# A feed-forward kernel whose second weight matrix is stored by even and odd columns and read back in alternation

## The chip, the core and the metric

The kernel runs on one core of one Trainium2 chip. The metric is the device time of one execution in microseconds (us). Before the change it is 949.09 us, the median of three runs (948.34 to 950.35).

## What is computed

Eight batches of eight heads, 576 tokens, head size 64. Half of the heads attend to the last 32 tokens, the other half to every 32nd token. The heads' outputs, side by side, are a row `x` of 512 numbers, and each row then goes through a normalised two-layer network with a residual:

```python
scores = where(mask_of_head, q @ k.T / 8, -1e9)
x = softmax(scores) @ v                     # [8, 576, 512] after joining the heads
xn = (x - mean(x)) / sqrt(var(x) + 1e-6) * g_ln
out = x + relu(xn @ w_ch1) @ w_ch2          # w_ch1 [512, 2048], w_ch2 [2048, 512]
```

The network is the larger part: 4608 tokens by 512 by 2048, twice.

## The kernel before

**Tiles and precision.** The 4608 tokens are cut into 9 chunks of 512 (`c`), the 2048 hidden columns into 16 blocks of 128 (`f`). Each weight and each activation is kept as two `fp32r` tiles, a high part and a low part that is the float32 value less the high part. A product of two such pairs takes three matmuls: high by high, low by high and high by low.

**One step `(c, f)`.** `ffn1` (L566 to L581) makes the 128 hidden columns of block `f` for the 512 tokens of chunk `c`: 12 matmuls into the PSUM tile `ph` (L575 eight, L579 four). ScalarE writes the high part `hh` (L563), VectorE the low part `hl` (L564). `ffn2` (L583 to L591) multiplies them by rows `128 f` to `128 f + 127` of the second matrix: for each of four blocks of 128 tokens three matmuls into `po`, `hh` by `w2h`, `hh` by `w2l`, `hl` by `w2h`, all on L589. In these the activations are the stationary operand (128 columns, loaded anew for each matmul) and the 512 columns of the second matrix are the moving operand, streamed past it. Over the whole program `ffn2` issues 9 x 16 x 12 = 1728 matmuls, and `ffn1` as many. `ffn2` of one step is issued after `ffn1` of the next, so that TensorE works while ScalarE and VectorE make `hh` and `hl`.

**Where the weight tiles come from.** The object `Split` turns each loaded block of the two matrices into the two parts. Its methods run on ScalarE (`scaled`, `low`), VectorE (`magnitude`, `sign`, `centred`) and GpSimd (`by_g`, `chunks_sum`). The last, `two_parts(i)`, makes the tile that the matmuls read: `i = 0` for the first matrix, `i = 1` for the second. ScalarE writes the high part (L241), GpSimd subtracts it from the full value to get the low part (L242). All 32 calls fall in the program's opening and in chunk 0; from chunk 1 on both matrices lie ready in SBUF. The tile of a block of the second matrix has 128 partitions by 2 parts by 512 columns of 4 bytes, so that one part is 2048 contiguous bytes in a partition.

**Attention.** The attention of the next batch (scores, exponentials, transposes and products of L375 to L472) is cut into pieces and placed, in a list written out by hand, between the matmuls of the network. Within each engine the instructions run in the order in which the program issues them.

**Names in the profile.** `po` is the accumulator of `ffn2`, `ph` that of `ffn1`; `w` is a weight tile of either matrix (L241 and L242 write it, 16 times each for each matrix); `r` is the weight's full value before the split; `xh` and `xl` are the two parts of the transposed activations, written on L489 and L491 with the tokens of the strided heads put back in order as they are written; `cm` is a small matmul of column means (L227), which waits for GpSimd's sum (L222).

Of the kernel before, what the change touches and what calls it, by code (L numbers as in the profile page):

```python
# [8 lines left out]
F32 = mybir.dt.float32  # L9
# [3 lines left out]
AF = mybir.ActivationFunctionType  # L13
ALU = mybir.AluOpType
# [6 lines left out]
def kernel(  # L21
# [10 lines left out]
    nc = tc.nc  # L32
# [50 lines left out]
    for jj in range(4):  # L83
        mrow = mask_l[STR * jj:STR * (jj + 1)]
        nc.gpsimd.affine_select(
            out=mrow, in_=mrow, pattern=[[1, 64]], base=-1,
            channel_multiplier=-1, compare_op=ALU.is_ge, fill=FILL)
        nc.gpsimd.affine_select(
            out=mrow, in_=mrow, pattern=[[-1, 64]], base=STR,
# [5 lines left out]
    for c in range(2):  # L95
        for r in range(3):
            msk = mask_s[64 * c:64 * (c + 1), NB * r:NB * (r + 1)]
            nc.gpsimd.affine_select(
                out=msk, in_=msk, pattern=[[-1, NB]], base=-NB * r,
                channel_multiplier=1, compare_op=ALU.is_ge, fill=FILL)  # L100
            nc.gpsimd.affine_select(
                out=msk, in_=msk, pattern=[[0, NB]], base=NB * r + NB - 1,
# [25 lines left out]
    def w_tile(i, f, shape, dtype, name):  # L128
        return w_pools[int(f >= NF2)].tile(shape, dtype, tag=f"w{i}_{f}", name=f"{name}{i}_{f}")
# [47 lines left out]

    staged, w1s, w2s = {}, {}, {}

    class Split:  # L180
        def __init__(self, f):
            self.f = f
            ws = staged.pop(f)
            self.bits = [t.rearrange("p (f t) -> p f t", t=2) for t in ws]
            self.bytes = [t.bitcast(U8).rearrange("p (f b) -> p f b", b=8) for t in ws]
            self.p, self.w = [None, None], [None, None]
# [47 lines left out]
        def two_parts(self, i):  # L234
            w = (self.wg, self.w[1])[i]
            t = w_tile(i + 1, self.f, [P, 2, DM], F32R, "w")
            (w1s, w2s)[i][self.f] = t
            if i == 1 and self.f == NFC - 1:

                w_pools[1].tile([P, PAD], F32, name="pad")  # L240
            nc.scalar.activation(out=t[:, 0], in_=w, func=AF.Copy)  # L241
            nc.gpsimd.tensor_tensor(out=t[:, 1], in0=w, in1=t[:, 0].bitcast(F32), op=ALU.subtract)  # L242

# [336 lines left out]

    def ffn2(c, f, h, po):  # L583
        hh, hl = h
        w2h, w2l = (w2s[f][:, i] for i in range(2))
        for i in range(NT):
            cs = slice(i * P, (i + 1) * P)
            for n, (hx, w) in enumerate(((hh, w2h), (hh, w2l), (hl, w2h))):
                nc.tensor.matmul(  # L589
                    po[i], hx[:, cs], w,  # L590
                    start=(f == 0 and n == 0), stop=(f == NFC - 1 and n == 2))  # L591
# [19 lines left out]
    a, b, c, d = first  # L611
# [110 lines left out]
    for c in range(NCHUNK):  # L722
# [18 lines left out]
        for f in range(NFC):  # L741
# [41 lines left out]
            if c == 0 and f == 1:  # L783
                ffn2(c, 0, prev, po)
# [6 lines left out]
            elif c + 1 == B:  # L791
                i = f // 2 - 1
# [9 lines left out]
            if prev is not None and (c or f > 1):  # L802
                ffn2(c, f - 1, prev, po)
# [6 lines left out]
            for i in scales.get(f, []):  # L810
                xres[i].append(x_scale(xres[i][0], f"{c}_{i}"))
            prev = h
        ffn2(c, NFC - 1, prev, po)
        finish(c, po, xres)

# [42 lines left out]
```

## Time and profile before

| | before |
|---|---|
| median of the runs | 949.09 us (948.34 to 950.35) |
| the profiled execution's own time | 949.45 us |
| its span, first to last instruction | 947.4 us |
| TensorE busy with matmuls | 916.7 us (97%) |
| VectorE, ScalarE, GpSimd busy | 388.9, 223.2, 143.4 us |
| mean granted TensorE clock | 0.993 |

A row of a group names line, engine, operation, output and input, the shape of both, the count, then busy time in us and the mean ns of one; behind the second bar stands the idle time of the engine just before these instructions and what ended it. Matmuls overlap in the pipeline, so the mean ns of one is longer than the distance from one to the next; distances are read from the starts in the timeline.

### The profile page before, as it was taken

To read this page: it belongs to the slowest core of one execution; us is meant where nothing else is said; L and a number is where in the kernel's file an instruction comes from. 1 tells how busy PE (TensorE), PEld (TensorE's weight loads), DVE (VectorE), ACT (ScalarE), POOL (GpSimd) and SP (SyncE) were. 2 spreads that over 40 slices of the span, in tenths; PEclk is the share of its full clock that TensorE was granted. 3 is DMA by queue.
4 is the path that set the end of the run, shared out by engine and by line. 5 is a ranking of instruction groups with operands and counts; after the bars stand their busy time and mean duration, and the time that the engine had idled before them with its cause. 6 is when DMAs were issued, how large, how long until landed. Compare 5 with 4: busy or idle time off the path is not lost.

```text
span 947.4 us, 18698 instructions
## 1 busy us (share of the span) xinstructions
PE 916.7 (97%) x7984; PEld 747.8 (79%) x7984; DVE 388.9 (41%) x685; ACT 223.2 (24%) x375; POOL 143.4 (15%) x180
## 2 busy tenths in 40 slices
PE   6589999999999999999999999999999999999996
PEld 5468877888888888888888888888888888888885
DVE  5768777334433344334433443334432331122112
ACT  4666751212111221111112112121112111111110
POOL 3477771000010001001100100000100000000000
PEclk9899999999999999999999999999999999999999
DMA  9999646424332352334253333243311130002001
GB/s 192 233 221 274 188 112 135 93 49 88 95 69 41 69 109 61 72 74 85 73 87 60 82 90 63 52 87 73 84 25 50 50 110 25 1 1 89 0 1 45
DMA packets 241666, 80.72 MB, mean 85 GB/s; under 512 B 192304, under 2 KB 234928, under 8 KB 241584
## 3 DMA queue, kind: packets, MB, share of 16 engines
q1 hardware_dynamic: 238688, 78.35, 36.5%
q10 hardware_dynamic: 2896, 1.18, 0.8%
q8 instruction: 63, 1.03, 0.5%
q14 instruction: 19, 0.16, 0.1%
HBM read 60.03 MB, written 19.46 MB: 84 GB/s over the span
## 4 chain that ended last, share of the span: by engine, by line
PE 92%; DVE 3%; DMA 2%; issue 1%; ACT 1%; SPq 1%; DVEq 0%; POOL 0%; POOLq 0%; ACTq 0%
PE po L589 41%; PE ph L575 27%; PE ph L579 13%; PE pp L416 2%; PE av L430 2%; PE px L472 2%; PE sp L387 2%; PE sp L375 1%; PE av L439 1%; DMA rows<-in_k_dram 1%; DMA raw<-in_q_dram 1%; DVE p L200 1%; PE t L315 1%; DVE r L206 1%; DVE x L595 0%
## 5 line engine op out<-in xcount | busy, mean ns | idle before, releaser
L589 PE MATMUL po<-w,hh 128*128 128x512 f32 x1152 | 367.6, 400 | 0.0
L564 DVE SCALAR_TENSOR_TENSOR hl<-ph,hh 128x512 fp32r<-128x512 f32 x144 | 99.5, 691 | 485.2 <-ACT hh L563 485.1
L589 PEld LDWEIGHTS po<-w,hh 128*128 128x128 f32 x1152 | 208.1, 188 | 42.3
L575 PE MATMUL ph<-xh,w 128*128 128x512 f32 x572 | 225.7, 395 | 4.8 <-DVE hl L564 4.8
L589 PE MATMUL po<-w,hl 128*128 128x512 f32 x576 | 225.5, 392 | 0.0
L575 PE MATMUL ph<-xl,w 128*128 128x512 f32 x572 | 223.6, 391 | 0.0
L563 ACT ACTIVATE hh<-ph 128x512 fp32r<-128x512 f32 x144 | 85.8, 596 | 557.7 <-PE ph L579 557.1
L579 PE MATMUL ph<-xh,w 128*128 128x512 f32 x572 | 153.3, 390 | 0.0
L575 PEld LDWEIGHTS ph<-xh,w 128*128 128x128 f32 x572 | 108.0, 189 | 27.4 <-DVE hl L564 5.0
L589 PEld LDWEIGHTS po<-w,hl 128*128 128x128 f32 x576 | 108.1, 188 | 24.4
L575 PEld LDWEIGHTS ph<-xl,w 128*128 128x128 f32 x572 | 108.0, 189 | 21.9
L579 PEld LDWEIGHTS ph<-xh,w 128*128 128x128 f32 x572 | 107.4, 188 | 22.4
L406 POOL TENSOR_TENSOR sm<-sm,mx 128x640 f32<-128x640 f32 (+1 forms) x32 | 40.6, 1270 | 432.5 <-DVE mx L401 432.5
L532 POOL TENSOR_TENSOR rs<-rs,mhalf 128x1 f32<-128x1 f32 x36 | 19.8, 549 | 326.0 <-DVE rs L531 326.0
L411 ACT ACTIVATE sm<-sm 128x640 f32<-128x640 f32 (+1 forms) x32 | 23.8, 743 | 98.8 <-POOL sm L406 98.7
L242 POOL TENSOR_TENSOR w<-r,w 128x512 fp32r<-128x512 f32 x32 | 41.2, 1295 | 24.0 <-ACT w L241 23.2
L491 DVE TENSOR_TENSOR xl<-px,xh 128x512 fp32r<-128x512 f32 (+2 forms) x48 | 30.1, 658 | 11.9 <-ACT xh L489 11.9
L595 DVE SCALAR_TENSOR_TENSOR x<-po,rs,x 128x512 f32<-128x512 f32 x36 | 24.8, 746 | 16.5 <-PE po L589 16.5
L489 ACT ACTIVATE xh<-px 128x512 fp32r<-128x512 f32 (+2 forms) x48 | 27.7, 654 | 9.7 <-PE px L472 9.0
L451 DVE TENSOR_TENSOR xo<-av,den 128x640 f32<-128x640 f32 (+1 forms) x32 | 28.5, 891 | 1.1
L200 DVE SCALAR_TENSOR_TENSOR p<-s,p 128x512 uint32<-128x512 uint32 x32 | 22.2, 693 | 12.3 <-ACT p L195 12.2
L401 DVE TENSOR_REDUCE mx<-sm 128x10 f32<-128x640 f32 (+1 forms) x32 | 26.4, 824 | 2.1
(77 smaller groups left out, 566.0 us busy)
## 6 DMA issues: line engine op xcount, KB each, us to landing
s<-in_moe_w_ch_dram SPq DMA_DIRECT2D x32, 512.0 KB
out_dram<-x SPq DMA_DIRECT2D x32, 256.0 KB
raw<-in_q_dram SPq DMA_DIRECT2D x112, 72.0 KB
raw<-in_k_dram SPq DMA_DIRECT2D x112, 72.0 KB
xds<-xo SPq DMA_DIRECT2D x32, 162.0 KB
v_l<-in_v_dram SPq DMA_DIRECT2D x32, 144.0 KB
v_l<-in_v_dram SPq DMA_DIRECT2D x32, 136.0 KB
xdl<-xo SPq DMA_DIRECT2D x16, 256.0 KB
```

The source lines that it names most:

```text
L200: nc.vector.scalar_tensor_tensor(out=self.p[i], in0=self.bits[i][:, :, 1], scalar=3, in1=self.p[i], op0=ALU.logical_shift_left, op1=ALU.bi ...
L242: nc.gpsimd.tensor_tensor(out=t[:, 1], in0=w, in1=t[:, 0].bitcast(F32), op=ALU.subtract)
L401: nc.vector.reduce_max(mx[:, :, 0:nt], sm, axis=AX.X)
L406: nc.gpsimd.tensor_tensor(out=sm, in0=sm, in1=mx[:, :, 0:nt].unsqueeze(3).broadcast_to([P, 2, nt, w]), op=ALU.subtract)
L451: nc.vector.tensor_tensor(out=xo[:, 0:nt].rearrange("p t h d -> p h t d"), in0=av[:, :, :, 0:D], in1=den.unsqueeze(3).broadcast_to([P, 2, ...
L489: nc.scalar.activation(out=dst(xh), in_=src, func=AF.Copy)
L491: nc.vector.tensor_tensor(out=dst(xl), in0=src, in1=dst(xh).bitcast(F32), op=ALU.subtract)
L563: nc.scalar.activation(out=hh, in_=ph, func=AF.Relu)
L564: nc.vector.scalar_tensor_tensor(out=hl, in0=ph, scalar=0.0, in1=hh.bitcast(F32), op0=ALU.max, op1=ALU.subtract)
L575: nc.tensor.matmul(ph, w1h[:, cc], x[:, cc, :], start=(n == 0), stop=False)
L579: nc.tensor.matmul(ph, w1l[:, cc], xh[:, cc, :], start=False, stop=(cc == NCC - 1))
L589: nc.tensor.matmul(po[i], hx[:, cs], w, start=(f == 0 and n == 0), stop=(f == NFC - 1 and n == 2))
```

## The change

Columns `2b` of a row of the second matrix are stored at place `b`, and columns `2b + 1` at place `256 + b`, in the high part and in the low part alike. `turns` gives the view of such a row that steps to and fro between the halves, so that element `2b + a` of the view is column `2b + a` of the matrix again. `two_parts(1)` writes both parts through this view, and reads the high part back through it; its source is read in its own order. `ffn2` streams the moving operand through the view. Each read or write goes 1024 bytes on, then 1020 back. The results, the PSUM tiles and the first matrix keep their order. No instruction is added, removed or moved on any engine; 16 instructions on ScalarE (L241), 16 on GpSimd (L242) and the 1728 matmuls of L589 get other addresses.

```diff
+    def turns(t):
+        return t.rearrange("p (a b) -> p b a", a=2)
...
         def two_parts(self, i):
...
-            nc.scalar.activation(out=t[:, 0], in_=w, func=AF.Copy)
-            nc.gpsimd.tensor_tensor(out=t[:, 1], in0=w, in1=t[:, 0].bitcast(F32), op=ALU.subtract)
+            hi, lo = t[:, 0], t[:, 1]
+            if i == 1:
+                w = w.rearrange("p (b a) -> p b a", a=2)
+                hi, lo = turns(hi), turns(lo)
+            nc.scalar.activation(out=hi, in_=w, func=AF.Copy)
+            nc.gpsimd.tensor_tensor(out=lo, in0=w, in1=hi.bitcast(F32), op=ALU.subtract)
...
     def ffn2(c, f, h, po):
         hh, hl = h
-        w2h, w2l = (w2s[f][:, i] for i in range(2))
+        w2h, w2l = (turns(w2s[f][:, i]) for i in range(2))
```

## The prediction

> **What bounds the kernel now.** I read the page's busy shares and the chain that ended last first, then the matmul groups, then the timeline of one step, and last the writes and copies whose shapes come nearest to the new ones. From the page:
>
> ```profile
> span 947.4 us, 18698 instructions
> PE 916.7 (97%) x7984; PEld 747.8 (79%) x7984; DVE 388.9 (41%) x685; ACT 223.2 (24%) x375; POOL 143.4 (15%) x180
> PE 92%; DVE 3%; DMA 2%; issue 1%; ACT 1%; SPq 1%; DVEq 0%; POOL 0%; POOLq 0%; ACTq 0%
> ```
>
> TensorE is the bound: 92% of the chain is its work. The groups of the changed matmuls, by shape:
>
> ```profile
> L589 PE MATMUL po<-w,hh 128*128 128x512 f32 x1152 | 367.6, 400 | 0.0
> L589 PE MATMUL po<-w,hl 128*128 128x512 f32 x576 | 225.5, 392 | 0.0
> ```
>
> 1152 + 576 = 1728 matmuls stream the second matrix, and TensorE never idles ahead of one. What one costs is its distance to the next, not its 400 ns. The timeline of a step in the middle of the program (start, length, engine, line):
>
> ```profile
> 502.24 0.39 PE L575 MATMUL ph<-xh,w 128*128 128x512 f32 x1
> 502.46 0.39 PE L575 MATMUL ph<-xl,w 128*128 128x512 f32 x1
> 502.69 0.39 PE L575 MATMUL ph<-xh,w 128*128 128x512 f32 x1
> 502.92 0.39 PE L575 MATMUL ph<-xl,w 128*128 128x512 f32 x1
> 503.14 0.39 PE L575 MATMUL ph<-xh,w 128*128 128x512 f32 x1
> ...
> 507.17 0.39 PE L589 MATMUL po<-w,hl 128*128 128x512 f32 x1
> 507.40 0.62 PE L589 MATMUL po<-w,hh 128*128 128x512 f32 x2
> 507.87 0.40 PE L589 MATMUL po<-w,hl 128*128 128x512 f32 x1
> 508.10 0.62 PE L589 MATMUL po<-w,hh 128*128 128x512 f32 x2
> 508.56 0.39 PE L589 MATMUL po<-w,hl 128*128 128x512 f32 x1
> 508.78 0.39 PE L575 MATMUL ph<-xh,w 128*128 128x512 f32 x1
> ```
>
> (503.14 - 502.24) / 4 = 0.225 us on L575, and (508.78 - 507.17) / 7 = 0.230 us on L589: about 227 ns for 512 columns, one column every 0.44 ns. No spare time stands between these matmuls. Whatever the new order of addresses adds to a column is added 512 x 1728 times, with nothing to hide it.
>
> **The change part by part.** No instruction is added, so there are three terms: the matmuls of L589, the 16 writes on ScalarE, the 16 subtractions on GpSimd.
>
> *The matmuls.* No TensorE operand of this trace is read with a step, so the price must be bounded. The lower end is nothing: the streaming reads may be fetched far enough ahead that addresses don't matter. A gain I leave out, since 227 ns is already what contiguous rows take on both lines. The upper end comes from the one place where this kernel visits far-apart elements of SBUF on another engine, the activations of the strided heads, whose 480 elements of a row are written 128 bytes apart. By shape, contiguous beside strided:
>
> ```profile
> L489 ACT ACTIVATE xh<-px 128x480 fp32r<-128x480 f32 x16 | 17.2, 1077 | 5.5 <-PE px L472 4.8
> L489 ACT ACTIVATE xh<-px 128x512 fp32r<-128x512 f32 x16 | 9.5, 595 | 4.2 <-PE px L472 4.2
> L489 ACT ACTIVATE xh<-px 128x32 fp32r<-128x32 f32 x16 | 4.6, 290 | 0.0
> L241 ACT ACTIVATE w<-r 128x512 fp32r<-128x512 f32 x32 | 20.0, 626 | 17.9 <-DVE r L230 16.5 <-DVE den L445 1.4
> L195 ACT ACTIVATE p<-s 128x512 uint32<-128x512 uint8 x32 | 20.5, 641 | 13.4 <-DVE r L206 13.1
> L330 ACT COPY qt_s<-t 64x288 f32<-64x288 f32 x8 | 3.2, 395 | 0.4 <-PE t L315 0.2
> L325 ACT COPY qt_l<-t 64x288 f32<-64x288 f32 x8 | 3.3, 411 | 4.1 <-PE t L315 3.9
> L491 DVE TENSOR_TENSOR xl<-px,xh 128x480 fp32r<-128x480 f32 x16 | 17.3, 1082 | 10.1 <-ACT xh L489 10.1
> L491 DVE TENSOR_TENSOR xl<-px,xh 128x512 fp32r<-128x512 f32 x16 | 10.9, 682 | 1.8 <-ACT xh L489 1.8
> ```
>
> Between the strided forms of 480 and 32 elements ScalarE pays (1077 - 290) / 448 = 1.76 ns an element. Between the contiguous forms, (595 - 411) / (512 - 288) = 0.82 ns. So far-apart writes to SBUF go at about half pace, and VectorE shows the same (480 take 1082 ns where 512 contiguous take 682). Small steps cost nothing: L195 reads every eighth byte at 641 ns, L325 writes every second element. And L330, which reads PSUM with a step of 16 elements and writes contiguously, is no slower than L325: that speaks for writes being what costs, and reads not. It is a read of PSUM, though, and the matmuls read SBUF.
>
> What would half pace be on TensorE? The trace shows the same matmul at half pace, early, where the granted clock is low (first the timeline, then a row of the windows view: stretch, length, busy us and counts, PEclk, DMA share, GB/s):
>
> ```profile
> 48.64 0.63 PE L575 MATMUL ph<-xh,w 128*128 128x512 f32 x1
> 49.06 0.63 PE L575 MATMUL ph<-xl,w 128*128 128x512 f32 x1
> 49.49 0.63 PE L575 MATMUL ph<-xh,w 128*128 128x512 f32 x1
> 49.92 0.63 PE L575 MATMUL ph<-xl,w 128*128 128x512 f32 x1
> ...
> 47.60:50.70 3.10, 3.08 (x7) 2.48 (x8) 2.73 (x4) 2.41 (x5) 2.36 (x3) 0.50 0.92 267
> ```
>
> At clock 0.50 the distance is (49.92 - 48.64) / 3 = 427 ns. So I take as half pace 427 ns a matmul, 200 ns more than now (227 ns more if all of today's 227 doubles). At the upper end, TensorE pays ScalarE's 1.76 ns for each column: 512 x 1.76 = 901 ns, 674 more. The ends are 0 and 674 ns a matmul. I take 200, because a factor of two is what both engines with rows pay, each against its own pace. The term is 1728 x 0.200 = 345.6 us.
>
> Here the Trainium skill speaks against the change. Its page "SBUF — State Buffer", section "Door 1: The DMA port swizzle", says that SBUF is fetched in 16-byte lines, that a line must be hit at least twice for full bandwidth, and that each step to a new line pays a penalty; it states no size. The trace agrees for writes of ScalarE and VectorE (1.76 against 0.82 ns, and no loss at 8-byte steps). By the rule every column of the new order opens another line and the term is above nothing; without it the term is nothing.
>
> *ScalarE.* 16 writes of 512 elements at the strided pace: 290 + 480 x 1.76 = 1135 ns instead of 626, 8.1 us in all if alternation costs what a long step costs, and nothing at the other end. GpSimd has no strided row; its bounds are nothing and a doubling:
>
> ```profile
> L242 POOL TENSOR_TENSOR w<-r,w 128x512 fp32r<-128x512 f32 x32 | 41.2, 1295 | 24.0 <-ACT w L241 23.2
> 47.00:66.00 19.00, 14.98 (x135) 11.59 (x136) 12.69 (x20) 12.46 (x21) 14.55 (x16) 0.90 0.94 202
> 66.00:157.00 91.00, 90.75 (x828) 73.88 (x827) 68.84 (x110) 53.87 (x90) 59.71 (x62) 1.00 0.75 187
> 60.60 2.56 POOL L242 TENSOR_TENSOR w<-r,w 128x512 fp32r<-128x512 f32 x2
> 65.06 0.45 POOL L222 TENSOR_TENSOR sum<-sum 128x128 f32<-128x128 f32 x1
> 65.56 0.49 PE L227 MATMUL cm<-sum,mean 128*128 128x128 f32 x2 [1.11 <-POOL sum L222]
> ```
>
> The last numbers before the clock are the busy times of ScalarE and GpSimd. From 66 us on, TensorE is full (90.75 of 91) and has GpSimd's 59.71 and ScalarE's 53.87 beside it: that cover hides both, and it grows when the matmuls get longer. Ahead of 66 us GpSimd is busy for 14.55 of 19 us and TensorE waits for it at 65.56 (1.11 us). A doubled L242 at 60.60 would hold that `cm` back by 1.3 us. But the 12 matmuls of L589 just ahead of it would take 12 x 0.2 = 2.4 us longer, so this 1.1 us of idle is absorbed, and GpSimd's delay is covered. For ScalarE I put 1.0 us on the path, two writes at half a microsecond each in the opening, where the chain runs through it.
>
> *Sum.* 345.6 - 1.1 + 1.0 = 345.5 us. Against the profiled execution's own 949.45 us (0.36 above the median) that gives 1295 us.
>
> **The rivals.**
>
> *Not slower: the reads are free.* If the moving operand is fetched well ahead, 227 ns stays. L330's stepped PSUM read speaks for it, and that the rows show the penalty only where something is written. Against it: at clock 0.50 the distance is 427 ns, so a matmul bound by the array alone would take 213 at full clock; it takes 227, so something that doesn't follow the array's clock is already near its limit. Left are ScalarE and GpSimd ahead of 66 us: 949.5 us if strides cost nothing there, 1.0 + 1.3 + 1.3 for two late sums makes 953, and 956 if GpSimd falls behind in chunk 0 too. The side turns at 1.1 ns a matmul (1.9 us over 1728). For this rival stands a sentence of the Trainium skill, page "TensorE: Matmul & The Clock Gate", section "Step-by-step: what each phase is for": "This is why throughput is purely `N cycles`". By it the sum would be this rival's; contiguous rows at two clocks bear it out only roughly (427 and 227), and no row here has a step.
>
> *Quarter pace: a column costs ScalarE's 1.76 ns.* Then a contiguous row is already at the limit: 227 ns / 128 groups of four columns is 1.77 ns a group, strikingly near to 1.76, and a step to a new place per column would cost one such group each. It gives 901 ns a matmul: 949.45 + 1728 x 0.674 = 2114 us; at twice the 427 ns, 854 a matmul, it is 2033 us. Against it: it takes ScalarE's time for TensorE's, and one coincidence.
>
> *In between.* If the alternation costs one more slot for each pair of columns, a matmul takes 1.5 x 227 = 340 ns: 949.45 + 1728 x 0.113 = 1145 us. Nothing in the rows speaks for a fraction.
>
> **How the numbers follow.** Half pace 0.33, with its own range from 1290 to 1345 us (200 to 227 ns a matmul). Quarter pace 0.30, 2030 to 2115 us. Free reads 0.22, 949 to 956 us. In between 0.15. The predicted time is half pace's 1295 us. No side case is small enough to be left out alone, so the range runs from 948 to 2115 us. A change of 0.2% (1.9 us) is about what a measurement of this kernel can tell from none. Of free reads I give 0.02 to faster, 0.12 to no change and 0.08 to slower; with the other three cases slower is 0.86.
>
> **What would show it.** Right: in the middle of the program the starts on L589 lie 427 ns apart, twelve take 5.1 us, while L575 keeps 227; the share of L589 in the chain goes from 41% to about 57%; TensorE still never idles ahead of L589, and its granted clock stays at 1.00 there. The ScalarE form of L241 for the second matrix reads near 1135 ns, GpSimd's between 1295 and 2590. Wrong: distances of 227 ns (free) or 850 to 900 (quarter pace) on L589; L575 slowed as well, which would mean something shared by both; or a lower granted clock in the middle.

## The result, and the profile after

The changed kernel takes 934.68 us (933.96 to 935.73, four runs) against 949.72 us for the kernel before in the same comparison: a ratio of 0.9836, with a 95% interval from 0.9824 to 0.9848. It is 15.0 us faster. The forecast was 1295 us, slower by a third; its range began at 948 us, so the result lies below all of it. The profiled execution took 934.81 us. Its page:

```profile
span 932.8 us, 18698 instructions
PE 899.6 (96%) x7984; PEld 750.0 (80%) x7984; DVE 391.2 (42%) x685; ACT 234.8 (25%) x375; POOL 145.2 (16%) x180
PE po L598 39%; PE ph L584 27%; PE ph L588 13%; PE pp L425 2%; PE av L439 2%; PE px L481 2%; PE av L448 1%; PE sp L396 1%; PE sp L384 1%; DMA xdl<-xo 1%; DVE r L210 1%; DMA rows<-in_k_dram 1%; DVE p L204 1%; PE cm L231 0%; DVE x L604 0%
```

TensorE is still the bound, and the share of the changed matmuls (now L598) fell from 41% to 39%. The timeline of a step in the middle, beside the one in the prediction:

```profile
494.66 0.38 PE L598 MATMUL po<-w,hl 128*128 128x512 f32 x1
494.88 0.59 PE L598 MATMUL po<-w,hh 128*128 128x512 f32 x2
495.31 0.38 PE L598 MATMUL po<-w,hl 128*128 128x512 f32 x1
...
496.61 0.38 PE L598 MATMUL po<-w,hl 128*128 128x512 f32 x1
496.82 0.40 PE L584 MATMUL ph<-xh,w 128*128 128x512 f32 x1
497.06 0.40 PE L584 MATMUL ph<-xl,w 128*128 128x512 f32 x1
```

Ten matmuls lie between 494.66 and 496.82: 216 ns each, where there were 230. In the chain of waits a step's groups stand merged (start, length, line, count), before and then after:

```profile
505.98 2.97 PE po L589 x12
508.95 1.81 PE ph L575 x8
```

```profile
500.58 2.79 PE po L598 x12
503.37 1.83 PE ph L584 x8
```

`ffn2` gains 0.18 us of 2.97. `ffn1`, which still reads straight rows, gives 0.02 back; why, no run here shows. When the work of a chunk ended is told by its last operation, the VectorE instruction that adds `po` to the residual, four of them in each chunk (shortest, median and longest ns, then the first and the last start in us), before and then after:

```profile
L595 DVE SCALAR_TENSOR_TENSOR x<-po,rs,x x36: 740/744/752, 159.4 to 941.0; 128x512 f32<-128x512 f32 x36
```

```profile
L604 DVE SCALAR_TENSOR_TENSOR x<-po,rs,x x36: 740/743/752, 161.5 to 926.3; 128x512 f32<-128x512 f32 x36
```

Chunk 0 ends 2.1 us later. From there to the last chunk it takes 764.8 us instead of 781.6, which is 16.8 us less over 8 x 192 = 1536 changed matmuls, or 10.9 ns for each. With 0.1 us at the end the span is 14.6 us shorter (947.4 to 932.8). Chunk 0, in which the tiles are made, gains nothing. The writers of the tile take longer there:

```profile
L251 POOL TENSOR_TENSOR w<-r,w 128x512 fp32r<-128x512 f32 x32 | 43.2, 1369 | 27.0 <-ACT w L250 25.0
L250 ACT ACTIVATE w<-r 128x512 fp32r<-128x512 f32 x32 | 27.2, 885 | 7.5 <-DVE r L234 5.9
```

Half of these 32 are unchanged (626 and 1295 ns before), so the alternating ones take 2 x 885 - 626 = 1144 ns on ScalarE and 2 x 1369 - 1295 = 1443 ns on GpSimd. TensorE waits longer for GpSimd's sums (line, releaser, total us, times, longest), 4.3 us where it was 1.1; before, then after:

```profile
PE cm L227 <- POOL sum L222: 1.1, 1, 1.1
```

```profile
PE cm L231 <- POOL sum L226: 4.3, 3, 3.0
```

The writers are only a part of this loss, as the experiments show. In this profile the granted clock was also lower between 47 and 66 us, 0.77 where the prediction's row of that stretch has 0.90 and the kernel that only stores the new way 0.88:

```profile
47.00:66.00 19.00, 15.34 (x129) 12.43 (x130) 12.74 (x20) 12.41 (x18) 14.12 (x14) 0.77 0.93 191
```

### The profile page after: what moved, and what is told of

Read it like the earlier page. It is cut to its first block, busy times and chain, and to the rows that moved or that the text cites. A ratio compares the mean times of both kernels' runs of the same rounds, so it can differ in the third digit from the quotient of the medians.

```text
span 932.8 us, 18698 instructions
## 1 busy us (share of the span) xinstructions
PE 899.6 (96%) x7984; PEld 750.0 (80%) x7984; DVE 391.2 (42%) x685; ACT 234.8 (25%) x375; POOL 145.2 (16%) x180
## 4 chain that ended last, share of the span: by engine, by line
PE 89%; DVE 3%; DMA 3%; issue 1%; ACT 1%; POOL 1%; SPq 1%; DVEq 0%; ACTq 0%; POOLq 0%
PE po L598 39%; PE ph L584 27%; PE ph L588 13%; PE pp L425 2%; PE av L439 2%; PE px L481 2%; PE av L448 1%; PE sp L396 1%; PE sp L384 1%; DMA xdl<-xo 1%; DVE r L210 1%; DMA rows<-in_k_dram 1%; DVE p L204 1%; PE cm L231 0%; DVE x L604 0%
## 5 line engine op out<-in xcount | busy, mean ns | idle before, releaser
L598 PE MATMUL po<-w,hh 128*128 128x512 f32 x1152 | 352.7, 388 | 0.0
L598 PEld LDWEIGHTS po<-w,hh 128*128 128x128 f32 x1152 | 209.1, 189 | 29.5
L598 PE MATMUL po<-w,hl 128*128 128x512 f32 x576 | 218.3, 379 | 0.0
L598 PEld LDWEIGHTS po<-w,hl 128*128 128x128 f32 x576 | 108.8, 189 | 15.4
L251 POOL TENSOR_TENSOR w<-r,w 128x512 fp32r<-128x512 f32 x32 | 43.2, 1369 | 27.0 <-ACT w L250 25.0
L250 ACT ACTIVATE w<-r 128x512 fp32r<-128x512 f32 x32 | 27.2, 885 | 7.5 <-DVE r L234 5.9
```

The lines of the kernel that those rows point to most:

```text
L250: nc.scalar.activation(out=hi, in_=w, func=AF.Copy)
L251: nc.gpsimd.tensor_tensor(out=lo, in0=w, in1=hi.bitcast(F32), op=ALU.subtract)
L598: nc.tensor.matmul(po[i], hx[:, cs], w, start=(f == 0 and n == 0), stop=(f == NFC - 1 and n == 2))
```

## The experiments

The question was what made a matmul faster by the order of its addresses, and whether it was the order at all. In all kernels but the second the matrix is stored in its natural order. `in_turn(t, (k, a, b, d))` is the view `p (k a b d) -> p k b a d`: a row is cut into `k` blocks, each block into `a` streams, each stream into `b` runs of `d` columns, and within a block the first runs of all streams are read, then the second runs. With (1, 2, 256, 1) it reads column b, then 256 + b. `PAT1` and `PAT2` give the pattern of each chunk for `ffn1` and `ffn2`. `undone` is the inverse on PSUM, and `plain` the natural view with matching dimensions.

**Only the reads.** `PAT2` is (1, 2, 256, 1) in every chunk, `PAT1` is empty.

```diff
-        w2h, w2l = (w2s[f][:, i] for i in range(2))
+        w2h, w2l = (in_turn(w2s[f][:, i], PAT2.get(c)) for i in range(2))
...
-                out=x, in0=po[i], scalar=rs, in1=x, op0=ALU.mult, op1=ALU.add)
+                out=plain(x, PAT2.get(c)), in0=undone(po[i], PAT2.get(c)), scalar=rs,
+                in1=plain(x, PAT2.get(c)), op0=ALU.mult, op1=ALU.add)
```

> The second matrix is stored in its natural order and only read in alternation (column b, then column 256+b), in all nine chunks; the last VectorE operation puts the columns of po back in order as it reads PSUM. Theory A (the order in which TensorE streams the moving operand is what gained): L589's matmuls stand 216 ns apart as in the changed kernel, against 227 before; 1728 x 10.8 ns = 18.7 us less than before, and no strided writes on ScalarE and GpSimd in the opening, so about 930.5 us, some 4 us under the changed kernel. Theory B (where the columns lie, or something else than the reads): 227 ns and about 949 us. Theory C (as A, but the stepped PSUM read of the last VectorE operation costs): 216 ns, that operation well above its 744 ns, time between 931 and 935.

Measured: 932.58 us, ratio 0.9818 (0.9805 to 0.9831). The groups of the matmul and of the VectorE operation, which reads PSUM with a step:

```profile
L615 PE MATMUL po<-w,hh 128*128 128x512 f32 x1152 | 352.7, 388 | 0.0
L621 DVE SCALAR_TENSOR_TENSOR x<-po,rs,x 128x512 f32<-128x512 f32 x36 | 24.5, 744 | 15.5 <-PE po L615 15.5
```

The mean of 388 ns is that of the changed kernel (400 before), the median distance of starts 216 ns, and the stepped PSUM read is free at 744 ns (746 before). Theory A holds: the order of the reads is the gain. The time came out 2 us above its 930.5, and 2 us under the changed kernel. The missing 2 us are lost in chunk 0 (the last operation of a chunk, then a row of the waits):

```profile
L621 DVE SCALAR_TENSOR_TENSOR x<-po,rs,x x36: 740/742/752, 159.1 to 923.8; 128x512 f32<-128x512 f32 x36
PE cm L250 <- POOL sum L245: 3.8, 2, 2.5
```

Chunk 0 ends 0.3 us sooner than in the kernel before, where its 192 matmuls should have saved 2.1 us, though no strided write stands in it. TensorE's wait for GpSimd's sums grew here too, from 1.1 to 3.8 us: where TensorE waits for other engines, faster matmuls bring little. From there on it takes 764.7 us, as in the changed kernel (764.8).

**Only the storage.** The changed kernel, but with straight reads:

```diff
-        w2h, w2l = (turns(w2s[f][:, i]) for i in range(2))
+        w2h, w2l = (w2s[f][:, i] for i in range(2))
...
-                out=x, in0=po[i], scalar=rs, in1=x, op0=ALU.mult, op1=ALU.add)
+                out=x.rearrange("p (b a) -> p b a", a=2), in0=turns(po[i]), scalar=rs,
+                in1=x.rearrange("p (b a) -> p b a", a=2), op0=ALU.mult, op1=ALU.add)
```

> The second matrix is stored with even columns first as in the changed kernel, but TensorE reads each row straight through; the last VectorE operation reorders po as it reads PSUM. Theory A: the matmuls are back at 227 ns, nothing is gained, and what the strided writes cost in the opening is seen alone: some 4 us, about 953 us (chunk 0 of the changed kernel ended 2.1 us later although its 192 matmuls should have saved 2.1). Theory B: 216 ns and about 935 us.

Measured: 951.62 us against 950.05, ratio 1.0016 (1.0007 to 1.0025).

```profile
L598 PE MATMUL po<-w,hh 128*128 128x512 f32 x1152 | 367.5, 400 | 0.0
L604 DVE SCALAR_TENSOR_TENSOR x<-po,rs,x x36: 741/744/752, 160.2 to 941.7; 128x512 f32<-128x512 f32 x36
```

The matmuls are back where they were. Storing in the new order costs 0.7 to 2.4 us by the interval, less than the 4 us expected; in the profile chunk 0 ends 0.8 us later than before.

**Both layers.** `PAT1` becomes (1, 2, 256, 1) in every chunk as well. The lines that it works on, against the kernel before (`pt` is `PAT1.get(c)`, `u` is `undone(ph, pt)`):

```diff
-                    ph, w1h[:, cc], x[:, cc, :], start=(n == 0), stop=False)
+                    ph, w1h[:, cc], in_turn(x[:, cc, :], PAT1.get(c)), start=(n == 0), stop=False)
...
-        nc.scalar.activation(out=hh, in_=ph, func=AF.Relu)
+        nc.scalar.activation(out=plain(hh, pt), in_=u, func=AF.Relu)
```

and likewise in the other matmuls of `ffn1` and in VectorE's operation for `hl`.

> As the read-only kernel, and ffn1 also reads its moving operand, the 512 tokens of a chunk, in alternation (token b, then 256+b); ScalarE and VectorE put ph back in order as they read PSUM. Theory A, if it holds for any moving operand: the 1728 matmuls of ffn1 go from 227 to 216 ns as well, another 18 to 19 us, about 912 us. If the gain belongs to the pair of tiles that ffn2 reads (second matrix against hh and hl): ffn1 stays at 227 ns and the time at about 930 us. If the stepped PSUM reads cost ScalarE and VectorE much: hh and hl come later, but a step of 6 us lies between them and their use, so no more than 1 us in all.

Measured: 914.63 us, ratio 0.9622 (0.9609 to 0.9635), the best of all: 18.0 us under the read-only kernel, 10.4 ns for each matmul of `ffn1`. The last operations of the chunks, then the chain of waits:

```profile
L621 DVE SCALAR_TENSOR_TENSOR x<-po,rs,x x36: 740/743/751, 162.1 to 906.4; 128x512 f32<-128x512 f32 x36
492.29 2.79 PE po L615 x12
495.08 1.73 PE ph L601 x8
```

Eight matmuls of `ffn1` take 1.73 us, 216 ns each. The gain belongs to the moving operands of both layers. After chunk 0 it is 20.4 us against the read-only kernel; chunk 0 itself, again without a strided write, ends 3.0 us later than there. At half the granted clock the same matmuls (timeline, then the windows view) show no gain:

```profile
47.91 0.63 PE L601 MATMUL ph<-xh,w 128*128 128x512 f32 x1
48.34 0.63 PE L601 MATMUL ph<-xl,w 128*128 128x512 f32 x1
48.77 0.63 PE L601 MATMUL ph<-xh,w 128*128 128x512 f32 x1
49.19 0.63 PE L601 MATMUL ph<-xl,w 128*128 128x512 f32 x1
...
47.40:49.50 2.10, 2.10 (x6) 1.65 (x5) 2.07 (x4) 1.74 (x3) 2.03 (x2) 0.50 1.02 292
```

(49.19 - 47.91) / 3 = 427 ns, as straight rows at that clock. If the array's own time halves as the clock doubles, it is 214 ns at full clock (an estimate from the 427). Of a straight row's 227 some 13 ns then don't follow the array's clock, and reading in turn takes 11 of them away.

**Many orders, first set.** Each chunk has a pattern of its own, (k, a, b, d), for `ffn1` and for `ffn2`:

```diff
+    PAT1 = {2: (128, 2, 2, 1), 3: (64, 2, 4, 1), 4: (32, 2, 8, 1), 5: (16, 2, 16, 1), 6: (8, 2, 32, 1), 7: (4, 2, 64, 1), 8: (2, 2, 128, 1)}
+    PAT2 = {2: (1, 2, 256, 1), 3: (1, 2, 128, 2), 4: (1, 2, 64, 4), 5: (1, 4, 128, 1), 6: (1, 16, 32, 1), 7: (1, 128, 4, 1), 8: (1, 256, 2, 1)}
...
+        w2h, w2l = (in_turn(w2s[f][:, i], PAT2.get(c)) for i in range(2))
```

> One look at many orders: each chunk from 2 to 8 reads its moving operands in an order of its own, chunks 0 and 1 straight through; the second matrix is stored naturally, and nothing is put back in order, so the outputs of chunks 2 to 8 come out permuted. ffn2, chunk 2: column b then 256+b, one each; chunk 3: two each; chunk 4: four each (16 bytes); chunk 5: four streams 512 bytes apart; chunk 6: sixteen streams 128 bytes apart; chunk 7: a constant step of 16 bytes; chunk 8: a constant step of 8 bytes. ffn1, two streams within short blocks: chunk 2: 8 bytes apart, 3: 16, 4: 32, 5: 64, 6: 128, 7: 256, 8: 512. Theory A1 (a straight row is held up because the next fetch comes from the place just fetched, and two places take turns): 216 ns in ffn2's chunks 2 and 5 and in ffn1 from some distance on, 227 at 8 bytes; single fetches without reuse (constant 16 bytes, sixteen streams) slow, 300 ns or more, as the prediction had feared for all. Theory A2 (any pattern with two dimensions is issued faster than a flat one): 216 ns in all of them, the distance of 8 bytes included. Theory A3 (the moving read collides with the weight load at certain addresses): no order by distance; ffn1 and ffn2 differ at the same distance.

This was one execution (1094.97 us). Median distance from one matmul's start to the next, by chunk; the two streams 8 to 512 bytes apart were read by `ffn1`, all other orders by `ffn2`:

| order of the columns | ns |
|---|---|
| straight (chunk 1, `ffn2` and `ffn1`) | 230, 227 |
| two streams in turn, 8 bytes apart (0, 2, 1, 3) | 227 |
| two streams, 16, 32, 64, 128, 256, 512 bytes apart | 216 each |
| two streams, 1024 bytes apart (the change's) | 216 |
| two from each half in turn | 334 |
| four from each half in turn | 254 |
| four streams | 283 |
| sixteen streams | 435 |
| constant step of 8 bytes; of 16 bytes | 451; 461 |

Rows of the timeline, for 8 bytes apart, two from each half, sixteen streams and a step of 16 bytes:

```profile
300.02 0.39 PE L601 MATMUL ph<-xh,w 128*128 128x512 f32 x1
...
301.16 0.39 PE L601 MATMUL ph<-xl,w 128*128 128x512 f32 x1
...
432.67 0.83 PE L615 MATMUL po<-w,hh 128*128 128x512 f32 x2
433.34 0.50 PE L615 MATMUL po<-w,hl 128*128 128x512 f32 x1
433.67 0.83 PE L615 MATMUL po<-w,hh 128*128 128x512 f32 x2
...
751.71 1.06 PE L615 MATMUL po<-w,hh 128*128 128x512 f32 x2
752.58 0.62 PE L615 MATMUL po<-w,hl 128*128 128x512 f32 x1
753.02 0.41 PE L601 MATMUL ph<-xh,w 128*128 128x512 f32 x1
...
901.59 1.11 PE L615 MATMUL po<-w,hh 128*128 128x512 f32 x2
...
903.89 0.65 PE L615 MATMUL po<-w,hl 128*128 128x512 f32 x1
904.36 0.40 PE L601 MATMUL ph<-xh,w 128*128 128x512 f32 x1
```

Five matmuls in 1.14 us, three in 1.00, three in 1.31, six in 2.77. A2 falls: orders with two dimensions run from 216 to 461. A3 falls only with the second set, where the same order costs the same in `ffn1` and in `ffn2`. A1, that far neighbours are what helps, expected 216 for four streams, which took 283, and it doesn't explain why two from each half are so much dearer than one.

**Many orders, second set.** What one from each half has in particular is that the even-numbered columns of the stream are one straight row and the odd-numbered another. That made theory L, against theory S, which kept the distance of neighbours. The edit adds two orders, each column `n` times and every `s`-th column of two halves in turn:

```diff
+        if pat[0] == "again":
+            n = pat[1]
+            return t[:, 0:512 // n].unsqueeze(2).broadcast_to([P, 512 // n, n])
+        if pat[0] == "far":
+            return t.rearrange("p (a b s) -> p s b a", a=2, s=pat[1])
```

> A second set of orders, made as the first (stored naturally, nothing put back, so chunks 1 to 8 don't give the reference's outputs; where columns repeat, others are left out). Theory L (two lanes): TensorE fetches even- and odd-numbered columns of the stream apart, and what counts is how many in a row each lane finds in one group of four neighbours: 4 in the change, 2 in a straight row, 1 in a step of 8 or 16 bytes. Theory S (same place): a straight row is held up because neighbours in the stream come from one place; any order whose neighbours lie far apart in two places is free of it. ffn2, chunk 1: the change's order, 216 ns by both. 2: two halves in turn, in each every second column (0, 256, 2, 258): L 227, S 216. 3: the same with every fourth: L 430 to 460, S 216. 4: each column twice (0, 0, 1, 1): L 216, S 227 or more. 5: eight streams: between the 283 of four and 435 of sixteen. 6: 32 streams, like sixteen. 7: each column four times: L 216, S 227 or more. 8: one column 512 times: the floor, 216. ffn1, orders that ffn2 had in the first set, and the same ns if the price belongs to the order: chunk 1 two from each half in turn, 334; 2 four from each, 250; 3 four streams, 283; 4 sixteen, 435; 5 a step of 16 bytes, 461; 6 of 8 bytes, 451; 7 every second column of two halves in turn, L 227, S 216; 8 each column twice, L 216, S 227.

Again this was one execution (1234.08 us).

| order | L | S | measured, ns |
|---|---|---|---|
| every second column of two halves, `ffn2`; `ffn1` | 227 | 216 | 228; 227 |
| every fourth column of two halves | 430 to 460 | 216 | 452 |
| each column twice, `ffn2`; `ffn1` | 216 | 227 or more | 216; 216 |
| each column four times | 216 | 227 or more | 216 |
| one column 512 times | 216 | - | 216 |
| eight streams; 32 streams | 283 to 435; 435 | - | 487; 434 |

In `ffn1` the orders of the first set gave 333, 251, 283, 434, 461 and 451: the price belongs to the order, not to the tile. Rows of the timeline, for every second column, every fourth, and each column twice:

```profile
349.80 0.39 PE L622 MATMUL po<-w,hl 128*128 128x512 f32 x1
...
352.07 0.41 PE L608 MATMUL ph<-xh,w 128*128 128x512 f32 x1
...
479.70 0.63 PE L622 MATMUL po<-w,hl 128*128 128x512 f32 x1
480.15 1.08 PE L622 MATMUL po<-w,hh 128*128 128x512 f32 x2
481.05 0.63 PE L622 MATMUL po<-w,hl 128*128 128x512 f32 x1
481.50 0.48 PE L608 MATMUL ph<-xh,w 128*128 128x512 f32 x1
...
625.51 0.38 PE L622 MATMUL po<-w,hl 128*128 128x512 f32 x1
...
627.02 0.59 PE L622 MATMUL po<-w,hh 128*128 128x512 f32 x2
```

Ten matmuls in 2.27 us, four in 1.80, seven in 1.51. S fails at all four orders on which the two differ, L holds at each. With each column twice, neighbours in the stream are the very same element, and it is fast; with every fourth column of two halves neighbours lie 1024 bytes apart, and it takes double. By these orders, what counts is how many columns in a row each of the two lanes, even and odd, finds in one group of four: four give 216 ns, two 227, one 450 to 460 (434 and 435 with sixteen and 32 streams). L isn't the whole account. It is wrong for eight streams. And where a lane leaves a group and comes back to it, its count gives 450 to 460 for two from each half and for four streams (one in a row) and 227 for four from each half (two in a row); they took 334, 283 and 254. That stays open.

## Why the prediction was wrong

- **What bounds the kernel** was right: TensorE before and after, and what an order does to one column is paid in full in chunks 1 to 8, in 1536 of the 1728 matmuls.
- **The step that failed** is the price of the matmuls: the lower end was set at nothing ("A gain I leave out, since 227 ns is already what contiguous rows take on both lines") and the value at +200 ns. After chunk 0 the mean distance from a matmul of `ffn2` to the next, over all starts of the two traces, fell from 234.8 to 221.5 ns, -13.3, and that of `ffn1` rose by 2.4: -10.9 net, where +200 was forecast. The kernel that only reads in turn shows that the order of the reads does it. The reasoning took each column as opening another group of elements. By the account of two lanes, which the second set of orders bears out in the main, it doesn't: for either lane the change turns "two in a row of every four" into a straight row.
- **The price itself was near for orders that do open a group with each column:** 435 to 487 ns against the 427 taken for half pace. That is no credit to the forecast, for the change is not such an order. The quarter pace fell: one group per column costs 451 / 512 = 0.88 ns, half of ScalarE's 1.76, and no run bears out the likeness of 1.77 and 1.76.
- **The clue was on the page.** The prediction saw that 227 is more than half of 427 and held it against free reads. It is an argument for a gain as much: an excess that doesn't follow the array's clock may be one that can be taken away. By that estimate 13.5 ns were there to win, and 11 were won.
- **The rules weighed.** The Trainium skill's page "SBUF — State Buffer", section "Door 1: The DMA port swizzle", asks for two hits on a 16-byte line. Counted per lane the runs agree in the main: one hit is dear (451 to 461 ns), two nearly free (227), though four are better still (216), and two from each half, with one hit at a time, cost 334. Its sentence on each step to a new line, read along the whole stream instead of per lane, led the wrong way. The page "TensorE: Matmul & The Clock Gate", section "Wait — 56ns, not 53.3ns?", gives 215.7 ns between matmuls of 512 columns at full clock; the new order reaches it (216), straight `fp32r` rows did not (227).
- **The writers.** ScalarE was right: 1135 ns forecast, 1144 measured. GpSimd's 1443 lies inside its bounds of 1295 and 2590. One reading was off: the 0.82 ns of the contiguous forms takes its 411 ns from L325, which writes every second element; with L330's 395 it is 0.89. The factor of about two stands either way.
- **The opening** was put at 1.0 us for the writers, and the storage-only kernel is near that: chunk 0 ended 0.8 us later in its profile, and its runs cost 0.7 to 2.4 us. What the sum left out is that chunk 0 keeps little of what faster matmuls save: 2.1 us were due, and the read-only kernel kept 0.3. The cover named for GpSimd (longer matmuls) wasn't there, and TensorE's wait for its sums grew. In the changed kernel chunk 0 ended 2.1 us later; how much of that is the lower clock of that profile (0.77 against 0.90) stays open.
- **The rival of free reads** had the matmuls at 227 ns and missed as well, on the same side.

## What to carry to other kernels

Compare the distance of matmuls at two clocks: where full clock takes more than its share of half clock, something beside the array's clock limits them, and here the order of reading won most of it back. For `fp32r` moving operands of 512 columns try reading one column from each of two places in turn (16 to 1024 bytes apart were tried), and undo the order where PSUM is read, which was free here (VectorE's last operation 744 ns against 746, ScalarE's `hh` 595 against 596); storing the operand in another order is then unneeded. Bound an untried access pattern from below zero too, and ask what the unit that reads it sees, not what the address list looks like.

## What the runs showed of the hardware

In most of the orders tried, TensorE behaved as if it fetched even- and odd-numbered columns of the `fp32r` moving operand in two lanes. Four neighbours in a row per lane took 216 ns for 512 columns, two (a straight row) 227, one 434 to 461, eight streams even 487. Two from each half in turn, which one would take for the gentler order, took 334, and four streams 283; by a count of hits in a row both should have taken 450 or more, so the two lanes are inferred and not the whole account. Each of these matmuls loads new weights; no run here shows what the orders cost without that. In the kernel before, straight rows of `ffn2`, which come right after a piece of attention work, ran at a median of 230 to 231 ns in chunks 1 to 6 and at 227 in chunks 7 and 8, and those of `ffn1` at 227; with reads in turn both have a median of 216.
